# Low halves of the even sequence pieces 76 to 90: a GpSimd subtraction in place of an accumulating transfer

## The chip, the cores and the metric

One core of one Trainium2 chip. The time is the device time of one execution in microseconds (us); the kernel before took 757.11 us, the median of three runs (753.76, 757.2 and 757.11). Less is better.

## The reference

The input `x` is one batch of 2048 positions by 640 channels. The output mixes two branches by a sigmoid gate:

```python
g = sigmoid((x * gate_w).sum(-1, keepdims=True))
# A: Fourier mixing, the real part of DFT_seq(DFT_hidden(x))
a = einsum("bsd,ed->bse", x, dft_hid_re)
b = einsum("bsd,ed->bse", x, dft_hid_im)
y = einsum("ts,bse->bte", dft_seq_re, a) - einsum("ts,bse->bte", dft_seq_im, b)
# B: 32 heads choose 2 of 256 experts by product keys
q = einsum("nd,dhc->nhc", x, w_q)           # halves q1, q2
s1, s2 = q1 @ k1.T, q2 @ k2.T               # 16 scores each
# the 2 best of each half, the 2 best of their 4 sums, softmax over these 2
act = gelu(einsum("nd,nhkd->nhk", x, u[top_e]))
out = einsum("nhk,nhk,nhkd->nd", softmax(top_s), act, v[top_e])
result = g * y + (1 - g) * out
```

## The kernel before, in words

Matrix products run on TensorE with 32-bit operands that are each the sum of a high half h (the value rounded to the short form `fp32r`) and a low half l = f - h. `mm3` (lines 143 to 145) makes three matmuls of each product: h by h, h by l and l by h. Every operand therefore needs a split: ScalarE writes h with a rounding copy (line 138), and VectorE or GpSimd writes l = f - h with a subtraction (line 139). The names of the profile: `wf` is the raw piece as it came from memory, `WS` holds the halves.

**The pieces.** The sequence transforms `wsre` and `wsim` are cut in 128 pieces of 128 rows by 512 columns; piece n is used in step n of the main loop (`seq_piece`). A step asks for piece n + 5 (`load_piece`, five buffers `wf`, queue SP), splits piece n + 3 (`split_piece`, four slots `WS`), and gives TensorE the 15 matmuls of piece n. Pieces 0 to 63 are the real part, 64 to 127 the imaginary part.

**Two ways to the low half.** Either `split` (lines 138 and 139): ScalarE writes h, GpSimd subtracts. Or the accumulating way (lines 188 to 191): ScalarE writes h (line 188), ScalarE writes -h into the slot of l (line 189), and a transfer issued from the GpSimd queue reads the piece from memory once more and adds it to that slot (line 191). A condition on n chooses. With `N0` = 30, `N1` = 66, `NT` = 16 and `ACCUM_END` = 92, the pieces 34 to 63 and the even ones from 76 to 90 go the accumulating way in the kernel before.

**What runs beside the pieces.** A `Pump` holds the background work of the other engines as generators; each yield tells an estimated time of VectorE, and after each group of matmuls `run_bg` takes as many of them as the time that TensorE has used allows. So the order of the instructions on every engine is fixed when the program is built; at run time the engines wait for one another by semaphores. From about piece 76 on, that work is `experts`: `build` makes three VectorE products of 128 x 1024 in 16-bit numbers (line 803, tiles `hot`, two or four sets of buffers), `use` multiplies three such sets on TensorE (48 small matmuls, line 815), `mask` scales their result on ScalarE (line 773), and `add_up` sums it on VectorE (line 779, tile `cd`). Before a build of a new set the sums of earlier ones are put in between, so VectorE waits for ScalarE at line 779, and TensorE for VectorE at line 815.

```python
for o, a, b, op in ((pt, row(0), wt, OP.is_equal), (qt, row(1), wt, OP.is_equal), (pt, pt, row(2), OP.mult)):
    nc.vector.tensor_tensor(o, a, b, op=op)
    yield (0.8 if early else 1.05) + settle()
```

`early` holds up to piece 91. The same ScalarE queue also carries `put_rows` (line 697), which empties a buffer into which SP's next transposing transfers (line 692) write, and SP's queue carries the loads of `wf` behind these. GpSimd also splits `draw` into `DD` (128 x 640, line 139) in this stretch.

Of the kernel before, what the change touches and what calls it, by code (L numbers as in the profile page):

```python
# [25 lines left out]
NT = S // P  # L26
# [17 lines left out]
ACCUM_END = NT * (NC + 2) - 4  # L44
# [62 lines left out]
def gated_mix_kernel(ctx: ExitStack, tc: tile.TileContext, xT, xn, dreT, dimT, wsre, wsim, wq, kT, uT, vv, gw, out):  # L107
# [28 lines left out]
    def split(f, h, l, eng):  # L136

        nc.scalar.activation(h, f, AF.Copy)  # L138
        eng.tensor_sub(l, f, h.bitcast(F32))  # L139
# [29 lines left out]
    N0 = 3 * NG + 6  # L169
# [11 lines left out]
    def split_piece(n):  # L181
        if n < NPC:
            psp[n] = h, l = WS[:, n % 4, 0], WS[:, n % 4, 1]
            f = pf.pop(n)
            if not N0 + 4 <= n < (4 * NT if n % 2 else ACCUM_END) or 4 * NT <= n < N1 + 10:
                split(f, h, l, nc.gpsimd)
                return
            nc.scalar.activation(h, f, AF.Copy)
            nc.scalar.activation(l, h.bitcast(F32), AF.Copy, scale=-1.0)  # L189
            w, c, s = pieces[n]  # L190
            nc.gpsimd.dma_start(l, (wsre, wsim)[w][c, s], accum_op=OP.add)  # L191
# [37 lines left out]
    def seq_piece(n):  # L229
        w, c, s = pieces[n]  # L230
        if s == 0:
            banks[:] = [bank(d) for d in range(KD)]
        load_piece(n + 5)
        split_piece(n + 3)
        h, l = psp.pop(n)
        if n < BYPASS:
            for a, (x, c) in enumerate(((0, h), (0, l), (1, h)) if n == 0 else ((0, h), (1, h), (0, l))):
                for d in range(KD):
                    nc.tensor.matmul(banks[d], X[s][:, x, d * P:(d + 1) * P], c, start=n + a == 0, stop=False)  # L239
            return  # L240
        for d in range(KD):
            ds = slice(d * P, (d + 1) * P)
            mm3(banks[d], X[s][:, 0, ds], X[s][:, 1, ds], h, l, s == 0, s == NT - 1)
            if s == NT - 1:
                staged[n // NT, d] = f = stage()
                nc.scalar.activation(f, banks[d], AF.Copy)
            run_bg(0.68)

    for q in range(2 * NC):
        n = NT * (q + 1)  # L250
# [66 lines left out]
    for n in (1, 2):  # L317
        split_x(n)
        split_piece(n)
# [158 lines left out]
    n = b + 2  # L478
# [254 lines left out]
    for p in range(NP):  # L733
        n = N0 + 4 * p + p // 2
        for a in range(4):
            at(n + 1 + a, score_step, p, a)
    N1 = n + 5
# [266 lines left out]
    for k, (n, m) in enumerate(((-1, 2), (0, 4), (5, 7), (7, 9), (10, 12))):  # L1004
        n, m = NT * (NC + 2) + n, NT * (NC + 2) + m
# [252 lines left out]
```

## Time and profile before

| | |
|---|---|
| runs | 753.76, 757.2, 757.11 us; median 757.11 |
| profiled execution | 755.74 us, of it the span of the profile 753.0 us |
| TensorE busy | 747.6 us (99%) |
| VectorE busy | 586.1 us (78%) |
| ScalarE busy | 361.3 us (48%) |
| GpSimd busy | 347.2 us (46%) |
| accumulating transfers | 30 of `wsre` and 8 of `wsim`, 256 KB each |

The span is what the profile sees between the first and the last instruction; 2.74 us of the profiled execution lie around it. All times inside the profile are counted from the start of the span. The eight accumulating transfers of `wsim` (pieces 76 to 90) are issued between 403.2 and 459.3 us. A row of the timeline gives the start, the duration, the engine, the line and the tiles of an instruction, and in brackets how long the engine stood idle before it and what ended that.

### The profile page before, as it was taken

What the parts mean: (1) busy time and instruction counts of PE and PEld (TensorE: products, weight loads), DVE (VectorE), ACT (ScalarE), POOL (GpSimd) and SP (SyncE); (2) the same over time, 40 slices, a digit from 0 to 9 for tenths busy, and PEclk for the clock granted to TensorE, in tenths of its full rate; (3) what the DMA queues carried; (4) which work ended last, traced back from release to release, by engine and by line L of the source; (5) the groups of instructions that cost most, each with busy time, mean ns of one, the idle gap of its engine ahead of it and who ended that gap; (6) DMA issues with size and microseconds to landing.
All of it is one profiled execution on the core that took longest, in us unless ns stands there. A gap on an engine that the chain in (4) does not pass through costs nothing.

```text
span 753.0 us, 11366 instructions
## 1 busy us (share of the span) xinstructions
PE 747.6 (99%) x4045; PEld 611.2 (81%) x4045; DVE 586.1 (78%) x741; ACT 361.3 (48%) x660; POOL 347.2 (46%) x286
## 2 busy tenths in 40 slices
PE   9999999999999999999999999999999999999998
PEld 7767777888888888888888887888888888888886
DVE  6964098278999999998999887979999974267651
ACT  4424134534345745653643687633545644443451
POOL 5533226352323423325345445644456793487252
PEclk9999999999999999999999999999999999999999
DMA  9999998568356776672496866478865789774301
GB/s 329 394 389 360 345 372 330 152 169 280 68 159 172 179 260 170 148 197 86 135 390 199 155 161 187 134 234 292 280 229 195 229 260 333 231 237 158 111 29 70
DMA packets 84488, 165.87 MB, mean 220 GB/s; under 512 B 16080, under 2 KB 23376, under 8 KB 84176
## 3 DMA queue, kind: packets, MB, share of 16 engines
q1 hardware_dynamic: 70960, 140.82, 55.7%
q0 software_dynamic: 5472, 9.96, 8.7%
q10 hardware_dynamic: 8000, 14.37, 5.2%
q8 instruction: 31, 0.51, 0.3%
q14 instruction: 25, 0.20, 0.1%
HBM read 132.46 MB, written 31.08 MB: 217 GB/s over the span
## 4 chain that ended last, share of the span: by engine, by line
PE 92%; DVE 3%; DMA 2%; ACT 1%; issue 1%; SPq 1%; ACTq 0%
PE b L143 29%; PE b L144 29%; PE b L145 29%; PE b L239 2%; PE b L365 2%; DMA wq<-in_wq 2%; PE b L815 1%; DMA wf<-in_wsim 1%; DVE ST L217 1%; DVE hot L803 1%; PE b L311 1%; ACT b L773 0%; SPq L692 0%; ACT WS L138 0%; DVE tw L139 0%
## 5 line engine op out<-in xcount | busy, mean ns | idle before, releaser
L143 PE MATMUL b<-WS,X 128*128 128x512 f32 x620 | 243.5, 393 | 0.0
L144 PE MATMUL b<-WS,X 128*128 128x512 f32 x620 | 241.5, 390 | 0.0
L145 PE MATMUL b<-WS,X 128*128 128x512 f32 x620 | 241.3, 389 | 0.0
L139 POOL TENSOR_TENSOR WS<-wf,WS 128x512 fp32r<-128x512 f32 x89 | 136.2, 1536 | 163.7 <-ACT WS L138 155.9
L143 PEld LDWEIGHTS b<-WS,X 128*128 128x128 f32 x620 | 116.4, 188 | 28.0 <-issue 3.6
L145 PEld LDWEIGHTS b<-WS,X 128*128 128x128 f32 x620 | 116.4, 188 | 24.5
L144 PEld LDWEIGHTS b<-WS,X 128*128 128x128 f32 x620 | 116.4, 188 | 23.3
L138 ACT ACTIVATE WS<-wf 128x512 fp32r<-128x512 f32 x89 | 55.6, 629 | 78.9 <-PE b L145 31.2
L139 POOL TENSOR_TENSOR WS<-ra,WS 128x512 fp32r<-128x512 f32 x39 | 55.3, 1430 | 14.9 <-ACT WS L138 14.5
L139 POOL TENSOR_TENSOR xl<-xf,xh 128x640 fp32r<-128x640 f32 x16 | 28.3, 1770 | 69.7 <-ACT xh L138 63.3
L138 ACT ACTIVATE WS<-ra 128x512 fp32r<-128x512 f32 x55 | 34.5, 631 | 50.9 <-PE b L145 34.6
L803 DVE TENSOR_TENSOR hot<-rows,wtab 128x1024 f16<-128x1024 f16 x64 | 57.7, 927 | 0.8 <-PE b L815 0.8
L548 ACT ACTIVATE sc<-b 128x512 f32<-128x512 f32 x32 | 19.2, 600 | 80.8 <-PE b L145 77.8
L191 POOL DMA_DIRECT2D WS<-in_wsre x30 | 26.4, 881 | 67.5 <-ACT WS L189 66.1
L773 ACT ACTIVATE b<-b,mask 128x128 f32<-128x128 f32 x128 | 43.0, 342 | 12.0 <-PE b L815 8.3
L139 POOL TENSOR_TENSOR WP<-ra,WP 128x512 fp32r<-128x512 f32 x18 | 26.4, 1482 | 43.2 <-ACT WP L138 43.1
L598 DVE TENSOR_TENSOR eq<-sc,mm 128x1024 f16<-128x1024 f32 x32 | 41.4, 1293 | 0.9
L605 DVE TENSOR_REDUCE tied<-eq 128x64 f32<-128x1024 f16 x32 | 39.0, 1218 | 0.9
L596 DVE TENSOR_REDUCE mm<-sc 128x64 f32<-128x1024 f32 x32 | 38.8, 1211 | 0.3
L779 DVE TENSOR_REDUCE cd<-b 128x128 f32<-128x512 f32 x32 | 21.7, 683 | 13.9 <-ACT b L773 9.7
L217 DVE SCALAR_TENSOR_TENSOR ST<-ST,grow 128x512 f32<-128x512 f32 x40 | 32.4, 872 | 0.1
L803 DVE TENSOR_TENSOR hot<-hot,rows 128x1024 f16<-128x1024 f16 x32 | 32.3, 1009 | 0.0
(203 smaller groups left out, 1480.0 us busy)
## 6 DMA issues: line engine op xcount, KB each, us to landing
wq<-in_wq SPq DMA_DIRECT2D x32, 640.0 KB, 7.0
X<-xd SPq DMA_DIRECT2D x30, 640.0 KB, 6.4
wf<-in_wsim SPq DMA_DIRECT2D x64, 256.0 KB, 4.7
wf<-in_wsre SPq DMA_DIRECT2D x63, 256.0 KB, 6.1
ra<-pd SPq DMA_DIRECT2D x47, 256.0 KB, 3.1
pd<-ST ACTq DMA_DIRECT2D x35, 256.0 KB, 5.3
WS<-in_wsre POOLq DMA_DIRECT2D x30, 256.0 KB, 5.4
xd<-X SPq DMA_DIRECT2D x9, 640.0 KB, 8.9
```

What stands on the lines that cost most here:

```text
L138: nc.scalar.activation(h, f, AF.Copy)
L139: eng.tensor_sub(l, f, h.bitcast(F32))
L143: nc.tensor.matmul(o, wh, ah, start=first, stop=False, skip_group_check=more)
L144: nc.tensor.matmul(o, wh, al, start=False, stop=False, skip_group_check=more)
L145: nc.tensor.matmul(o, wl, ah, start=False, stop=last, skip_group_check=more)
L191: nc.gpsimd.dma_start(l, (wsre, wsim)[w][c, s], accum_op=OP.add)
L217: nc.vector.scalar_tensor_tensor(f, f, -1.0 if w else 1.0, g, op0=OP.mult, op1=OP.mult)
L596: nc.vector.tensor_reduce(m, sc, op=OP.max, axis=AX.X)
L598: nc.vector.tensor_tensor(eq, sc, m[:, :, None].to_broadcast([P, HH, E]), op=OP.is_equal)
L605: nc.vector.tensor_reduce(tied[:, s, ib, :], eq, op=OP.add, axis=AX.X)
L773: nc.scalar.activation(f[:, :, n], f[:, :, n], AF.Copy, scale=mask4[:, n:n + 1])
L803: nc.vector.tensor_tensor(o, a, b, op=op)
```

## The change

The condition in `split_piece` is replaced by a shorter one. Pieces 34 to 63 still go the accumulating way; the even pieces from 76 to 90 are now split as their odd neighbours are, by ScalarE's rounding copy and GpSimd's subtraction.

```diff
-            if not N0 + 4 <= n < (4 * NT if n % 2 else ACCUM_END) or 4 * NT <= n < N1 + 10:
+            if not N0 + 4 <= n < 4 * NT:
                 split(f, h, l, nc.gpsimd)
                 return
             nc.scalar.activation(h, f, AF.Copy)
             nc.scalar.activation(l, h.bitcast(F32), AF.Copy, scale=-1.0)
             w, c, s = pieces[n]
             nc.gpsimd.dma_start(l, (wsre, wsim)[w][c, s], accum_op=OP.add)
```

`ACCUM_END` keeps its value and still ends `early`. The order of TensorE's and VectorE's instructions stays as it was; the rows of two engines change.

On GpSimd, at the pieces 76 to 80 (`WS` the low half, `wf` the raw piece, `DD` the split of `draw`), before (-) and now (+):

```order
-L191 DMA WS<-in_wsim 128x512
-L139 TENSOR_TENSOR WS<-wf,WS 128x512
+L139 TENSOR_TENSOR WS<-wf,WS 128x512 x2
 L139 TENSOR_TENSOR DD<-draw,DD 128x640
-L191 DMA WS<-in_wsim 128x512
-L139 TENSOR_TENSOR WS<-wf,WS 128x512
-L191 DMA WS<-in_wsim 128x512
+L139 TENSOR_TENSOR WS<-wf,WS 128x512 x3
 L139 TENSOR_TENSOR DD<-draw,DD 128x640
```

Each transfer has become a subtraction at the same place in the queue, so that two or three subtractions now stand between two splits of `DD`.

On ScalarE, at piece 76 (line 138 the rounding copy that makes h, line 188 the same copy in the accumulating way, line 189 its copy with the sign turned):

```order
 L138 ACTIVATE WS<-wf 128x512 x3
 L138 ACTIVATE DD<-draw 128x640
-L188 ACTIVATE WS<-wf 128x512
-L189 ACTIVATE WS<-WS 128x512
+L138 ACTIVATE WS<-wf 128x512
 L666 ACT_TABLE_LOAD
 L666 ACTIVATE cc<-cc 128x128
```

The copy with the turned sign is gone here, and in the same way at the other seven pieces; nothing else in the queue has moved.

## The prediction

> **What bounds the kernel now.** I read the page first, then the busy time by windows around the eight changed pieces, then who waits for whom there, then the timelines of the five engines.
>
> ```profile
> PE 747.6 (99%) x4045; PEld 611.2 (81%) x4045; DVE 586.1 (78%) x741; ACT 361.3 (48%) x660; POOL 347.2 (46%) x286
> 402.00:422.00 20.00, 20.00 (x104) 16.33 (x103) 19.59 (x36) 7.94 (x13) 10.40 (x8) 1.00 0.94 212
> 422.00:442.00 20.00, 20.00 (x174) 16.47 (x167) 15.58 (x25) 17.06 (x37) 8.90 (x7) 1.00 0.55 123
> 442.00:462.00 20.00, 20.00 (x176) 16.25 (x175) 15.38 (x22) 15.72 (x30) 6.99 (x6) 1.00 0.80 234
> 462.00:482.00 20.00, 19.41 (x129) 15.76 (x128) 20.00 (x19) 12.77 (x32) 16.93 (x11) 1.00 0.32 87
> PE b L815 <- DVE hot L803: 0.6, 1, 0.6
> DVE cd L779 <- ACT b L773: 8.9, 4, 4.2
> ```
>
> TensorE is the bound: 747.6 of 753.0 us. The columns of a window are its length, then TensorE, its weight loads, VectorE, ScalarE, GpSimd, the granted clock, the DMA share and GB/s. From 402 to 462 us TensorE has no idle time at all, and the clock is full. So nothing that is taken off another engine there can be won on TensorE, except the one wait of 0.6 us for VectorE's `hot` near 471 us. But VectorE is nearly as full: 19.59 of 20 before 422 us, then two windows with room, which is its 8.9 us of waiting for ScalarE's masks, and 20.00 of 20 after 462 us. The question is what the change does to VectorE, and whether TensorE notices.
>
> **What the change removes.** Eight copies with turned sign on ScalarE and eight transfers issued by GpSimd.
>
> ```profile
> L189 ACT ACTIVATE WS<-WS x38: 631/633/635, 132.2 to 458.2; 128x512 fp32r<-128x512 f32 x38
> L191 POOL DMA_DIRECT2D WS<-in_wsim x8: 863/888/903, 403.2 to 459.3; - x8
> DMA to landing us min/median/max: 4.1/4.8/7.8
> ```
>
> That is 8 x 0.63 = 5.1 us of ScalarE, 8 x 0.89 = 7.1 us of GpSimd, and 8 reads of 256 KB. ScalarE's share lies beside TensorE's work except in one chain (below). A piece is also ready sooner, since a subtraction replaces a transfer that lands 4.8 us later, but TensorE never waited for these pieces, so that is worth nothing.
>
> **What it adds.** Eight GpSimd subtractions of 128 x 512.
>
> ```profile
> L139 POOL TENSOR_TENSOR WS<-wf,WS x89: 1280/1533/2344, 8.1 to 589.5; 128x512 fp32r<-128x512 f32 x89
> 412.43 1.51 POOL L139 TENSOR_TENSOR WS<-wf,WS 128x512 fp32r<-128x512 f32 x1 [1.53 <-ACT WS L138]
> 412.11 2.39 DVE L803 TENSOR_TENSOR hot<-rows,wtab 128x1024 f16<-128x1024 f16 x2
> 415.02 1.28 DVE L803 TENSOR_TENSOR hot<-rows,wtab 128x1024 f16<-128x1024 f16 x2
> 425.32 0.90 POOL L191 DMA_DIRECT2D WS<-in_wsim  x1 [4.36 <-ACT WS L189]
> 425.64 1.28 DVE L803 TENSOR_TENSOR hot<-rows,wtab 128x1024 f16<-128x1024 f16 x2
> ```
>
> GpSimd itself has room: 8 x 1.53 = 12.2 us less the 7.1 removed. VectorE pays. Two products of line 803 take 1.28 us when GpSimd is quiet (415.02), and also while it issues a transfer (425.64); they take 2.39 us when a GpSimd subtraction runs beside them (412.11). So each subtraction costs VectorE 1.11 us, a transfer's issue nothing. From below the cost of one is 0, where VectorE idles or runs an instruction that isn't blocked:
>
> ```profile
> 463.37 3.44 POOL L139 TENSOR_TENSOR WS<-wf,WS 128x512 fp32r<-128x512 f32 x2
> 463.87 0.68 DVE L779 TENSOR_REDUCE cd<-b 128x128 f32<-128x512 f32 x1
> ```
>
> The sum of line 779 keeps its 0.68 us inside two subtractions. The Trainium skill, "SBUF — State Buffer", section "Who interferes with whom", has the rule that speaks against this change: a VectorE instruction with two inputs in SBUF contends with a GpSimd instruction that reads SBUF, a reduction doesn't, and the loser is blocked until the other has finished. The rows agree on who is blocked; on the length they show 1.11 us, where a whole undisturbed subtraction lasts 1.28. With 1.28 for each the result below would be 2.9 instead of 2.4 us.
>
> **The first group: three subtractions that nothing absorbs.** Pieces 76, 78 and 80 are split while VectorE works without a gap towards the first `use`.
>
> ```profile
> 400.39 1.56 POOL L139 TENSOR_TENSOR DD<-draw,DD 128x640 fp32r<-128x640 f32 x1
> 400.45 1.78 DVE L609 TENSOR_TENSOR first<-tied,top_bits 128x256 int32<-128x256 int32 x1
> 401.51 0.63 ACT L188 ACTIVATE WS<-wf 128x512 fp32r<-128x512 f32 x1 [2.14 <-issue]
> 403.40 0.42 DVE L609 TENSOR_TENSOR tied<-tied,top_bits 128x256 int32<-128x256 int32 x1
> 408.31 0.63 ACT L188 ACTIVATE WS<-wf 128x512 fp32r<-128x512 f32 x1 [1.41 <-POOL WS L139]
> 409.86 0.95 DVE L671 RECIPROCAL cc<-cc 128x128 f32<-128x128 f32 x1
> 415.06 0.63 ACT L188 ACTIVATE WS<-wf 128x512 fp32r<-128x512 f32 x1 [2.72 <-PE b L145]
> 416.22 0.68 DVE L803 TENSOR_TENSOR hot<-hot,rows 128x1024 f16<-128x1024 f16 x1
> 419.73 1.78 DVE L803 TENSOR_TENSOR hot<-hot,rows 128x1024 f16<-128x1024 f16 x1
> 421.75 0.95 PE L815 MATMUL b<-hot 128*64 128x64 f16 x48
> 422.63 0.50 PE L143 MATMUL b<-WS,X 128*128 128x512 f32 x1
> ```
>
> The three rows of line 188 give the moment from which each subtraction can start. Piece 76 (402.14 on) meets small VectorE operations with two inputs; line 609 shows that they are blocked too (1.78 us beside a split of `DD`, 0.42 without), so 1.1. Piece 78 (408.94 on, and behind 77 and a split of `DD` in GpSimd's queue, so nearer 410) meets mostly one-input operations such as the reciprocal, for which no row shows a block: between 0 and 1.1, and I take 0.5. Piece 80 (415.69 on) meets line 803: 1.1. VectorE is then 1.1 + 0.5 + 1.1 = 2.7 us late. The third set of the first group was finished at 419.73 + 1.78 = 421.51 us; its 16 matmuls are the last third of the 48 that fill 421.75 to 422.63, so they began at 422.34. Slack 0.8 us. TensorE waits 2.7 - 0.8 = 1.9 us.
>
> **The middle: absorbed.** Pieces 82 to 88 cost VectorE up to 4.4 us more, but it had 8.9 us of waiting there, and the waits are set by ScalarE, whose masks follow TensorE's own matmuls. The longest of them ends a chain:
>
> ```profile
> 436.94 1.47 ACT L773 ACTIVATE b<-b,mask 128x128 f32<-128x128 f32 x4 [1.25 <-PE b L815]
> 439.79 0.63 ACT L189 ACTIVATE WS<-WS 128x512 fp32r<-128x512 f32 x1
> 443.08 1.93 ACT L697 ACTIVATE rows<-lb 128x384 f16<-128x384 f16 x1
> 445.04 3.64 SPq L692 DMA_TRANSPOSE lb<-lb  x3
> 448.72 2.58 SPq L177 DMA_DIRECT2D wf<-in_wsim  x4
> 454.28 0.63 ACT L138 ACTIVATE WS<-wf 128x512 fp32r<-128x512 f32 x1 [3.49 <-DMA wf<-in_wsim]
> 456.30 0.69 DVE L779 TENSOR_REDUCE cd<-b 128x128 f32<-128x512 f32 x1 [4.18 <-ACT b L773]
> ```
>
> TensorE's second group frees ScalarE at 436.94; ScalarE then works without a gap to line 697 (443.08), SP's transposes wait for that (445.04), the next load of `wf` stands behind them (448.72), ScalarE waits for it (454.28), and its masks release VectorE (456.30). In the changed kernel this chain starts 1.9 us late with TensorE and loses the 0.63 us of one copy (439.79). VectorE restarts 1.3 us late whatever it lost in between.
>
> **The end of the stretch.** From there VectorE has no gap until TensorE's wait:
>
> ```profile
> 457.57 0.62 ACT L188 ACTIVATE WS<-wf 128x512 fp32r<-128x512 f32 x1
> 469.26 1.77 DVE L803 TENSOR_TENSOR hot<-hot,rows 128x1024 f16<-128x1024 f16 x1
> 471.09 0.44 PE L815 MATMUL b<-hot 128*64 128x64 f16 x16 [0.59 <-DVE hot L803]
> ```
>
> Piece 90 (458.19 on) meets line 803 again and adds 1.1, so the set that ended at 469.26 + 1.77 = 471.03 comes 1.3 + 1.1 = 2.4 us later. TensorE waited for it already before, so it now goes on 2.4 us later than before; 1.9 of this it had lost at the first group. Behind this place all engines are late by the same amount, and TensorE, full, gives nothing back.
>
> **The sum.** +2.4 us. On the profiled execution (753.0 of span and 2.74 around it, 755.74) that makes 758.1; the median of the runs lies 1.4 higher, and the measured time is a median, so I give 757.1 + 2.4 = 759.5. The unknown prices move it from +0.8 (of these only pieces 80 and 90 block: 1.1 - 0.8 = 0.3 at the first group, 0.3 - 0.6 = -0.3 at the chain, -0.3 + 1.1 = 0.8 at the end) to +3.0 (piece 78 at its full 1.1).
>
> **Rivals.** *Nothing is absorbed.* VectorE becomes the bound for the whole stretch: the subtractions stack up, all eight at 1.1 us, 8.8 less the 0.8 of slack, +8.0 us, which is 763.7 on the profiled execution. For it: 20.00 of 20 after 462 us, and the estimated 0.8 us per `build` instruction, less than the 0.88 us that VectorE's row group
>
> ```profile
> L803 DVE TENSOR_TENSOR hot<-rows,wtab 128x1024 f16<-128x1024 f16 x28 | 23.7, 879 | 0.0
> ```
>
> shows on average even with the transfers. Against it: the 8.9 us of waiting in between. It passes 0.5% (3.8 us) once five of the eight reach TensorE, since 5 x 1.1 - 0.8 = 4.7: the three of the first group at full price and two of the last, for instance where the wait for `wf` at 454 us is shorter and VectorE's gap of 4.18 us goes. *The cover holds.* The early subtractions fall on unblocked operations and the removed copies bring the chain forward by 0.6 us: the wait at 471.09 goes, -0.6 us, 755.1 on the profiled execution. Against it: line 803 at pieces 80 and 90. *The transfers were in the way.* Without the accumulating reads the loads of `wf` come sooner and the slower runs become like the fastest, 753.8. Against it: TensorE stands still for just 0.59 us in the whole stretch, so the profile offers no such gain. That the change does nothing is excluded: GpSimd's and ScalarE's queues differ at eight places.
>
> **Chances.** A measurement of this kernel tells about 0.5%, 3.8 us, from no change. My case, +0.3 to +3.8 us: 0.44. Nothing or less absorbed, over +3.8 us: 0.42, high because each further blocked instruction of line 803 in the full windows goes straight into TensorE's wait, and because every error of my count that I can name (a second subtraction beside the same build, less waiting at line 779) points that way. The cover holds: 0.08. The transfers were in the way: 0.06. So slower by over 0.5% 0.42, within it 0.44 + 0.08 = 0.52, faster 0.06. The range goes from 755.1, the cover's time, to 763.7, the time of the rival without absorption; it leaves out the faster case and what of the slower one lies higher.
>
> **What would show it.** In the profile after: TensorE's wait for `hot` at the first use of line 815 near 422 us, about 1.9 us, and a second, 0.5 to 1.1 us long, near 473 us; line 803's mean between 402 and 462 us above 0.88 us; VectorE's wait at line 779 shorter than 8.9 us; line 773 released by the load of `wf` near 456 us; the stretches before 402 and after 480 us unchanged in length. Wrong it is if TensorE's first wait is missing, if waits appear at the groups near 436 or 448 us, or if TensorE's idle time grows where no line 815 stands.

## The result, and the profile after

The changed kernel takes 758.07 us in the median of 18 runs (756.42 to 760.92), the kernel before 754.81 us in the median of 18 (753.76 to 758.09): a ratio of 1.0038, 95% interval 1.0027 to 1.0049, or +2.9 us (2.0 to 3.7). It is slower, by less than the 0.5% that the prediction took as its bound. The forecast was +2.4 us, inside the interval. As a time it was 759.5 us, 1.4 too long, since it was counted from the median of only three runs of the kernel before, 757.11 us, which lies 2.3 above the median of all 18. The profiled execution took 757.59 us with a span of 755.8.

The first line of the page after, and the four windows of the prediction (length, then TensorE, weight loads, VectorE, ScalarE, GpSimd, granted clock, DMA share, GB/s):

```profile
PE 748.3 (99%) x4045; PEld 611.7 (81%) x4045; DVE 596.1 (79%) x741; ACT 356.6 (47%) x652; POOL 350.9 (46%) x286
402.00:422.00 20.00, 20.00 (x90) 16.57 (x89) 19.59 (x31) 6.53 (x10) 12.78 (x9) 1.00 0.58 183
422.00:442.00 20.00, 18.64 (x169) 14.99 (x168) 20.00 (x26) 13.18 (x28) 8.10 (x5) 1.00 0.21 60
442.00:462.00 20.00, 20.00 (x151) 16.18 (x151) 20.00 (x23) 16.64 (x32) 11.88 (x8) 1.00 0.69 225
462.00:482.00 20.00, 19.13 (x165) 15.65 (x159) 20.00 (x21) 11.97 (x31) 13.70 (x9) 1.00 0.31 87
```

VectorE is busy for 10.0 us more in all, though its instructions are the same 741, and from 422 to 482 us it has no idle time left; before, it had 9.0 us of it between 422 and 462. TensorE has lost 1.36 us in the second window. Where, the timeline of TensorE shows, at the first group of line 815 and at the fifth:

```profile
422.67 0.83 PE L815 MATMUL b<-hot 128*64 128x64 f16 x32
424.86 0.44 PE L815 MATMUL b<-hot 128*64 128x64 f16 x16 [1.36 <-DVE hot L803]
472.31 0.69 PE L815 MATMUL b<-hot 128*64 128x64 f16 x32
473.88 0.44 PE L815 MATMUL b<-hot 128*64 128x64 f16 x16 [0.87 <-ACT b L773]
```

Two thirds of the first group run at once, the last third waits for VectorE's product. Without the wait it would have begun 0.59 us after the group, at 423.26; so the group loses 1.6 us. At the fifth group the wait of before, 0.59, has grown to 0.87. (The name behind it, line 773, is the last release in the profile; VectorE's product ended at 473.83.) These two places make about 1.8 us of the 2.8 between the two spans. The rest lies ahead of any changed instruction, in TensorE's waits for `wq` at the start of the kernel: 0.9 us here, 0.4 in the profile before, and 0.5 us within the first 6 us.

### The profile page after: what moved, and what is told of

It reads as the page before. It is cut to its first block, busy times and chain, and to the rows that moved or that the text cites. A ratio compares the mean times of both kernels' runs of the same rounds, so it can differ in the third digit from the quotient of the medians.

```text
span 755.8 us, 11360 instructions
## 1 busy us (share of the span) xinstructions
PE 748.3 (99%) x4045; PEld 611.7 (81%) x4045; DVE 596.1 (79%) x741; ACT 356.6 (47%) x652; POOL 350.9 (46%) x286
## 4 chain that ended last, share of the span: by engine, by line
PE 85%; DVE 12%; DMA 2%; issue 1%; ACT 0%; SPq 0%; DVEq 0%
PE b L143 27%; PE b L144 26%; PE b L145 26%; PE b L239 2%; PE b L365 2%; DMA wq<-in_wq 2%; DVE eq L598 1%; DVE mm L596 1%; DVE hot L803 1%; PE b L815 1%; DVE ST L217 1%; DVE eq L603 1%; DVE tied L605 1%; DVE sc L601 1%; PE b L311 1%
## 5 line engine op out<-in xcount | busy, mean ns | idle before, releaser
L139 POOL TENSOR_TENSOR WS<-wf,WS 128x512 fp32r<-128x512 f32 x97 | 146.9, 1519 | 174.8 <-ACT WS L138 173.0
L138 ACT ACTIVATE WS<-wf 128x512 fp32r<-128x512 f32 x97 | 60.7, 629 | 87.2 <-PE b L145 35.7
L803 DVE TENSOR_TENSOR hot<-rows,wtab 128x1024 f16<-128x1024 f16 x64 | 67.5, 1080 | 0.8 <-PE b L815 0.8
L143 PE MATMUL b<-WU,xh 128*128 128x512 f32 x80 | 31.2, 391 | 0.0
```

The lines of the kernel that those rows point to most:

```text
L143: nc.tensor.matmul(o, wh, ah, start=first, stop=False, skip_group_check=more)
```

## The experiments

Each ran in rounds with the kernel before on the same chip. "Lost" below is how much later TensorE's instructions start than in a trace of the kernel before, counted only behind 400 us, so that the start of the kernel is left out.

**Both kernels once more.**

> The changed kernel unaltered, for a second trace. The first trace shows 1.6 us lost at the first group and 0.2 us more near 474 us, 1.8 us in all, where the medians differ by 2.9 us. If the missing 1.1 us lies at the same two places in other executions, this trace shows over 2.2 us there; if they repeat to 0.3 us, the rest is in the transfers at the start of the kernel, which differ between executions. Ratio 1.003 to 1.005.

> The kernel before unaltered, for a second trace. Ratio 1.000. No wait at the first group near 422 us; the wait near 471 us of 0.6 us either repeats or shows how much it differs between executions; the waits for wq between 107 and 121 us differ by more than that.

The changed kernel: 758.18 us, ratio 1.0046 (1.0032 to 1.0061). The kernel before against its own other runs: 1.0009 (0.9998 to 1.0021). TensorE in the second trace of the changed kernel, and then in the second trace of the kernel before, at the fifth group:

```profile
424.02 0.84 PE L815 MATMUL b<-hot 128*64 128x64 f16 x32
426.22 0.44 PE L815 MATMUL b<-hot 128*64 128x64 f16 x16 [1.36 <-DVE hot L803]
473.81 0.55 PE L815 MATMUL b<-hot 128*64 128x64 f16 x24
475.16 0.44 PE L815 MATMUL b<-hot 128*64 128x64 f16 x16 [0.81 <-DVE hot L803]
```

```profile
470.82 0.95 PE L815 MATMUL b<-hot 128*64 128x64 f16 x48
```

The first group's wait repeats, 1.36 us in both. The wait at the fifth group is not a fixed part of the kernel before: 0.59 in its first trace, none in its second. Between the second traces the changed kernel loses 1.6 us at the first group and 1.0 at the fifth, 2.6 in all; between the first traces it was 1.8. The second lies inside the measured +2.0 to +3.7 us, the first 0.2 below it. TensorE's waits for `wq` were 2.1 and 1.0 us in this pair; they are what differs most between executions, and a remainder of 0.3 to 1 us isn't told apart from them.

**One part of the change alone.** In `e1_first` the condition ends `4 * NT <= n < N1 + 16`, in `e2_last` the even pieces go the accumulating way up to `N1 + 16`:

```diff
-            if not N0 + 4 <= n < (4 * NT if n % 2 else ACCUM_END) or 4 * NT <= n < N1 + 10:
+            if not N0 + 4 <= n < (4 * NT if n % 2 else ACCUM_END) or 4 * NT <= n < N1 + 16:   # e1_first
+            if not N0 + 4 <= n < (4 * NT if n % 2 else N1 + 16) or 4 * NT <= n < N1 + 10:     # e2_last
```

> Pieces 76, 78 and 80 by subtraction as in the changed kernel, 82 to 90 by accumulating transfers as before. Lock theory (each GpSimd subtraction blocks a two-input VectorE operation for 1.1 us, and TensorE loses only where a set of hot falls due): TensorE's wait at the first group near 423 us is there, about 1.6 us; VectorE is set right again by ScalarE's masks in the middle; +1.6 us on the kernel before. Even-share rival (each of the eight costs the same part of the measured 2.9 us): 3 x 0.37 = +1.1 us, and no particular wait. Transfer rival (the loss comes with the transfers and copies that are taken away): also 3 x 0.37 = +1.1 us, with a wait that is not at line 815.

> Pieces 76, 78 and 80 by accumulating transfers as before, 82 to 90 by subtraction as in the changed kernel. Lock theory: no wait at the first group; five locks of 1.1 us fall into VectorE's 8.9 us of waiting at line 779, so TensorE's wait near 471 us grows from 0.6 to between 0.9 and 1.7 us: +0.3 to +1.1 us. Even-share rival: 5 x 0.37 = +1.8 us.

`e1_first` 757.59 us, ratio 1.0035 (1.0022 to 1.0049); `e2_last` 756.14 us, ratio 1.0013 (1.0001 to 1.0025). TensorE's waits for VectorE, first in `e1_first`, then in `e2_last` (us in total, times, longest):

```profile
PE b L815 <- DVE hot L803: 1.4, 1, 1.4
```

```profile
PE b L815 <- DVE hot L803: 1.2, 1, 1.2
```

In `e1_first` it is the wait at the first group, with the same 1.36 us and 1.55 lost; the fifth group has no wait, as in the second trace of the kernel before. In `e2_last` the first group has no wait, and the one at the fifth is 1.18 us: 0.5 lost against the first trace of the kernel before, which waits there too, and 1.4 against the second, which doesn't. By the runs, three of the eight subtractions cost +2.6 us (1.7 to 3.7) and the other five +1.0 (0.1 to 1.9). An even share would have made it +1.1 and +1.8. The first figure speaks against the even-share rival, the second is too wide to; more telling is that each wait stands at the group behind its own pieces and at no other. The figure of `e1_first` is 1 us above what was expected; its trace shows no more than the expected loss behind 400 us, and long waits for `wq` (3.1 us) ahead of any changed instruction, so that difference stays open.

**The subtraction without taking anything away, and taking away without the subtraction.** In `e3_dummy` (first part of the diff) a subtraction is added ahead of each of the eight transfers; in `e4_none` (second part) the eight low halves are left out.

```diff
+            if n >= 4 * NT:
+                nc.gpsimd.tensor_sub(f, f, h.bitcast(F32))
             nc.gpsimd.dma_start(l, (wsre, wsim)[w][c, s], accum_op=OP.add)
...
+            if n >= 4 * NT:
+                return
             nc.scalar.activation(l, h.bitcast(F32), AF.Copy, scale=-1.0)
```

> The kernel before with all of its transfers and copies, and beside each of the eight accumulating transfers of pieces 76 to 90 one more GpSimd subtraction of 128 x 512, whose result (written over the raw piece) nobody uses. Lock theory: what is added is the whole cost: +1.9 to +2.9 us, with a wait of 1.6 us or a little more at the first group. Transfer rival: nothing is taken away, so 0.

> The low halves of the even pieces 76 to 90 are left out: neither transfer, nor copy with turned sign, nor subtraction; the slots keep older low halves. Lock theory: no lock and less on ScalarE, so between -0.6 us (the wait near 471 us goes) and 0. Transfer rival: the loss comes with what is taken away, so about +2.9 us.

`e3_dummy` 759.49 us, ratio 1.0057 (1.0045 to 1.0069), +4.3 us; `e4_none` 755.45 us, ratio 1.0004 (0.9994 to 1.0014), no difference that can be measured. Adding the subtractions alone makes the kernel slower, taking the transfers and copies away alone does nothing that can be measured: the transfer rival falls. But `e3_dummy` costs more than expected, and not all of it is the subtractions' price. TensorE's waits in it, by line and cause (two lines were added above, so line 817 is the former 815 and 805 the former 803):

```profile
PE b L817 <- DVE hot L805: 1.7, 2, 1.0
PE b L144 <- DMA WS<-in_wsim: 1.1, 1, 1.1
```

The second wait is new: the transfers now stand behind the added subtractions in GpSimd's queue, one of them landed too late for its piece, and TensorE stood 1.15 us for it near 420 us and lost 1.4. That one isn't VectorE's, and it takes part of what the first group's wait would have been (0.73 us there). Without these 1.4 us the trace has lost 1.5 us behind 400 us against the first trace of the kernel before and 2.4 against the second, which is near the changed kernel's loss. The changed kernel has no such transfers.

**More of the same.** `e6_double` makes each of the eight subtractions twice:

```diff
                 split(f, h, l, nc.gpsimd)
+                if n % 2 == 0 and 4 * NT + 12 <= n < ACCUM_END:
+                    nc.gpsimd.tensor_sub(f, f, h.bitcast(F32))
                 return
```

> The changed kernel with each of the eight GpSimd subtractions made twice, the second over the raw piece and unused. Lock theory with slack: VectorE has no idle time left from 422 us on in the changed kernel, so each of the eight further locks of 1.1 us reaches TensorE: 8 to 9 us over the changed kernel, +10 to +12 us on the kernel before; the first group's wait rises from 1.4 to about 4.5 us. Even-share rival: twice the loss, +5.8 us.

766.21 us, ratio 1.0161 (1.0139 to 1.0183), +12.2 us: far from twice 2.9, so the second lock costs much more than the first, as when the slack is used up. The first group's three waits add to 4.9 us (1.07, 1.36 and 2.43; the lines stand two further down here too). But the sum came out as expected partly for another reason. Behind the longest wait TensorE itself ran slow (matmuls at the first group and after, then windows with the granted clock in the third column from the end):

```profile
429.72 0.64 PE L817 MATMUL b<-hot 128*64 128x64 f16 x16 [2.43 <-DVE hot L805]
430.29 0.80 PE L143 MATMUL b<-WS,X 128*128 128x512 f32 x1
430.88 0.63 PE L144 MATMUL b<-WS,X 128*128 128x512 f32 x1
```

```profile
426.00:430.00 4.00, 0.72 (x26) 0.61 (x28) 4.00 (x6) 1.47 (x4) 2.31 (x2) 0.90 0.25 74
430.00:434.00 4.00, 4.00 (x23) 3.17 (x20) 4.00 (x6) 1.19 (x2) 0.79 (x1) 0.50 0.23 66
434.00:438.00 4.00, 4.00 (x15) 3.19 (x14) 2.75 (x5) 2.50 (x5) 0.00 (x1) 0.75 0.00 0
```

Counted in the trace, 8.4 us are lost in waits for VectorE and 4.3 us in stretches at half clock behind waits of 2.43 and 2.35 us. So the waits grew from about 2.6 to 8.4 us, 5.8 for eight further locks, less than the 8 to 9 expected: while TensorE was slow, VectorE found idle time again (one wait of 3.1 us at the former line 779).

**Another engine for the subtraction.** `e5_vector` puts the eight on VectorE:

```diff
-                split(f, h, l, nc.gpsimd)
+                split(f, h, l, nc.vector if n % 2 == 0 and 4 * NT + 12 <= n < ACCUM_END else nc.gpsimd)
```

> The eight subtractions of the changed kernel on VectorE in place of GpSimd. A VectorE subtraction of this size takes 0.69 us in the trace, 0.6 from start to start; a GpSimd one blocks VectorE for 1.1 us. Lock theory: VectorE is late by 3 x 0.6 = 1.8 us at the first group instead of 2.4, less 0.8 of slack: a wait of 1.0 us there, and +0.5 to +1.5 us in all, less than the changed kernel. Rival (the place in VectorE's queue matters, since it must wait for ScalarE's copy): VectorE stands still at line 139 and it is slower than the changed kernel, +3 us or more.

757.35 us, ratio 1.0033 (1.0021 to 1.0045), +2.5 us, above the expected +0.5 to +1.5 and not told apart from the changed kernel. The lines of VectorE in it between 400 and 465 us (minimum, median and maximum in ns), and what it waited for:

```profile
L139 DVE TENSOR_TENSOR WS<-wf,WS x8: 677/680/1787, 410.4 to 457.2; 128x512 fp32r<-128x512 f32 x8
DVE WS L139 <- ACT WS L138: 2.2, 2, 1.4
```

Six of the eight take the expected 0.68 us, and the first group's wait is 0.60 us with 0.8 lost instead of 1.6. But two, at 413 and 441 us, meet other GpSimd work and take 1.79 and 1.64 us, and VectorE twice stood waiting for ScalarE's copy at its own subtraction, 2.2 us. TensorE lost another 0.5 us at the group near 449 us, and at the one near 471 us 1.0 against the second trace of the kernel before, 0.2 against the first. The rival had part of it right: the place in the queue takes back some of what the lower price gives.

**What a GpSimd instruction with one input costs.** In `e8_one_input` GpSimd multiplies h by -1 in place of the subtraction, so that the low halves of these pieces hold -h:

```diff
+                if n % 2 == 0 and 4 * NT + 12 <= n < ACCUM_END:
+                    nc.scalar.activation(h, f, AF.Copy)
+                    nc.gpsimd.tensor_scalar(l, h.bitcast(F32), -1.0, None, op0=OP.mult)
+                    return
                 split(f, h, l, nc.gpsimd)
```

> The changed kernel with the eight GpSimd subtractions replaced by a GpSimd multiplication of h by -1, which reads one tensor in place of two and writes the same 128 x 512 (so the low halves of these eight pieces hold -h). Lock theory with the block lasting as long as GpSimd reads: blocks of about half the length if the time follows the number of tensors read, a wait of under 0.5 us at the first group and 0 to +1 us in all; if any GpSimd instruction that reads blocks for 1.1 us, +2.9 us as in the changed kernel; if an instruction with one input doesn't block, 0.

756.52 us, ratio 1.0020 (1.0008 to 1.0032), +1.5 us, and no wait at the first group. GpSimd's instruction at piece 80 and VectorE's two products beside it (line 807 is the former 803):

```profile
416.15 1.94 POOL L188 TENSOR_SCALAR WS<-WS 128x512 fp32r<-128x512 f32 x1 [2.11 <-ACT WS L187]
416.06 1.70 DVE L807 TENSOR_TENSOR hot<-rows,wtab 128x1024 f16<-128x1024 f16 x2
```

The two take 1.70 us, where an undisturbed pair takes 1.28 and a pair beside a subtraction 2.39. So this instruction blocks VectorE for 0.42 us against 1.11, though it lasts no less long itself; beside six of the eight, one operation of VectorE is longer by 0.41 to 0.43 us. The price does not follow the length of GpSimd's instruction. That it follows the number of tensors read is likely and not shown alone, since the operation is another one too. Of the +1.5 us the trace shows 0.2 behind 400 us against the first trace of the kernel before and 1.1 against the second, there at the fifth group (a wait of 0.74 us); the rest stays open.

**Taking more away.** `e7_more` lets six more even pieces, 92 to 102, go the accumulating way (`ACCUM_END + 12` in the condition).

> The kernel before, with the even pieces 92 to 102 by accumulating transfers too, six more than before. Lock theory: six locks of 1.1 us less between 463 and 500 us, but TensorE there waits for VectorE only 0 to 0.6 us, so -0.6 to 0 us. Rival (each lock that is taken away gives its share, 0.37 us): -2.2 us.

755.56 us, ratio 1.0005 (0.9993 to 1.0017). Its trace has no wait of TensorE at line 815 at all, and that brings nothing that can be measured: the second trace of the kernel before has none either. No version here beats the kernel before.

## Why the prediction was right, point by point

**The bound.** TensorE stays the bound; its lost time is the result. Right.

**The price of a subtraction.** 1.11 us on VectorE was right where a blocked operation lies beside the whole subtraction; three of the last five, which fall in part on the sums of line 779, cost 0.5 to 0.7 us. That the removed transfers and copies are worth nothing was right (`e4_none`).

**The first group.** VectorE's operations at pieces 76 and 78 in the profile after, with GpSimd's subtraction of 78 between them:

```profile
403.19 1.52 DVE L626 TENSOR_TENSOR tied<-tied,first 128x256 f32<-128x256 f32 x1
411.24 1.34 POOL L139 TENSOR_TENSOR WS<-wf,WS 128x512 fp32r<-128x512 f32 x1
411.36 1.45 DVE L660 COPY lb<-lb 128x256 f16<-128x256 f16 x2
412.98 0.95 DVE L671 RECIPROCAL cc<-cc 128x128 f32<-128x128 f32 x1
416.94 1.78 DVE L803 TENSOR_TENSOR hot<-hot,rows 128x1024 f16<-128x1024 f16 x1
424.13 0.68 DVE L803 TENSOR_TENSOR hot<-hot,rows 128x1024 f16<-128x1024 f16 x1
```

Piece 76 cost 1.1 (line 626 took 0.42 before), piece 80 another 1.1 (line 803, 0.68 before), both as predicted. Piece 78, put at 0.5, cost its full 1.1: it met the 16-bit copy of line 660, whose two copies took 0.35 us before and now 1.45. The subtraction of piece 79 began at 413.33, inside the reciprocal, which took its 0.95 as before. With the start of the kernel 0.92 us later, the third set ended at 424.81 instead of 422.43: 2.4 us late, not 3.3, because the shift let two other locks fall on cheaper places. So the sum of 2.7 was 0.3 too high, the slack of 0.8 was right, and the wait, predicted as 1.9 us, was 1.6.

**The middle.** This step failed. The prediction let VectorE restart at line 779 when ScalarE's masks came, behind the late load of `wf`. The row that answers to 456.30:

```profile
454.86 0.63 ACT L138 ACTIVATE WS<-wf 128x512 fp32r<-128x512 f32 x1 [1.02 <-DMA wf<-in_wsim]
455.79 0.68 DVE L779 TENSOR_REDUCE cd<-b 128x128 f32<-128x512 f32 x1
```

ScalarE waits 1.02 us for `wf` instead of 3.49, and VectorE doesn't wait at line 779 at all, here or at any other place of the stretch: its 8.9 us of waiting are gone. The locks of the last five subtractions don't fill them alone. Between the first and the fifth group, 18 operations of VectorE are longer than the shortest of their kind, each of them beside a subtraction of GpSimd, by 17.2 us together; in the kernel before it was 8.1 us. The five new subtractions make only 3.9 us of this, since three of them fall in part on those sums. The other 13.3 us, 5 more than before, come from GpSimd work that the change leaves alone. One case, first in the kernel before, then in the changed one:

```profile
428.06 1.55 POOL L139 TENSOR_TENSOR DD<-draw,DD 128x640 fp32r<-128x640 f32 x1 [1.83 <-ACT DD L138]
429.87 0.69 DVE L779 TENSOR_REDUCE cd<-b 128x128 f32<-128x512 f32 x1 [2.35 <-ACT b L773]
```

```profile
430.28 1.85 POOL L139 TENSOR_TENSOR DD<-draw,DD 128x640 fp32r<-128x640 f32 x1 [3.72 <-ACT DD L138]
430.04 2.65 DVE L803 TENSOR_TENSOR hot<-rows,wtab 128x1024 f16<-128x1024 f16 x2
```

Before, this split of `DD` ran while VectorE waited and cost it nothing; now it meets two products and costs 2.65 - 1.28 = 1.37 us. So VectorE's idle time had hidden locks of the old work, and the prediction, which counted only the new ones, had no term for these. VectorE is the late one from then on: of the 2.4 us carried in, 1.9 are left at the fifth group. The chain that was worked out in such detail does not set the time there. Where the last five subtractions are missing, in `e1_first`, VectorE still waits 6.2 us at line 779 and TensorE doesn't wait at the fifth group: there the step holds.

**The fifth group.** Predicted +0.5 us beyond the first group's 1.9; the traces show +0.2 and +1.0 beyond 1.6. The size was near, the way to it was not: that the sum came out near the measured +2.9 us is in part luck. And the predicted range of +0.8 to +3.0 us hid that the wait of 0.59 us before was itself no constant.

**The rivals.** *Nothing is absorbed* (+8.0) is refuted for eight locks, but the idle time that spoke against it is used up: `e6_double` shows what the next eight do. *The cover holds* and *the transfers were in the way* are refuted by `e3_dummy` and `e4_none`.

## What to carry to other kernels

Where VectorE runs close behind TensorE, a GpSimd instruction beside it is to be priced by what it takes from VectorE, not by GpSimd's own busy share: a subtraction of 128 x 512 here cost VectorE 1.1 us, more than the 0.68 us that the same subtraction takes on VectorE. Count such locks from the last place where VectorE had idle time to the next place where TensorE needs its result, and take off the slack there; three of the eight pieces made most of this loss. Where the new locks use up VectorE's idle time, count also the old locks that it had hidden. And take a second trace of the kernel before: a wait that is in one and not in the other is no term of a sum.

## What the runs showed of the hardware

Two things were not expected. First, a GpSimd instruction that lasts 1.94 us blocked VectorE for 0.42 us when it read one tensor, while one that lasts 1.3 to 1.5 us and reads two blocked it for 1.1. The Trainium skill, "SBUF — State Buffer", section "SBUF: two separate sides", says that the loser is blocked for the whole instruction; here the block was shorter than the instruction as the profile shows it in both cases, and the measured prices stand. The Trainium skill, on the same page, section "Who interferes with whom", names copies among the operations that can take part in it, which the two copies of line 660 bear out.

Second, TensorE's granted clock fell to half after single waits of 2.03 us and more, but not after those of up to 1.6 us (the longest, 1.61 us for `wq` in `e6_double`, kept the full clock). Beside the two cases of `e6_double`, two of the waits for `wq` at the start show it, one of 2.06 us in `e1_first` and here the one in `e4_none`, with windows of 4 us:

```profile
109.05 1.07 PE L367 MATMUL b<-wq,kp 128*32 128x320 f32 x8 [2.03 <-DMA wq<-in_wq]
108.00:112.00 4.00, 2.95 (x13) 1.74 (x14) 3.42 (x9) 1.90 (x6) 0.00 (x0) 0.67 0.90 323
112.00:116.00 4.00, 4.00 (x17) 3.22 (x16) 1.36 (x3) 1.58 (x5) 0.85 (x1) 0.91 0.81 268
```

The two windows lack 0.33 and 0.09 of the clock; at half clock that is 2 x 4 x 0.42 = 3.4 us. The three windows of `e6_double` give 2 x 4 x (0.10 + 0.50 + 0.25) = 6.8 us in the same way, two such stretches. The Trainium skill, "TensorE: Matmul & The Clock Gate", section "HAM oscillation — how this bites in real kernels", puts the limit at gaps of about 3.4 us; here a gap of 2.03 us was enough. What lies between 1.6 and 2.0 us, and whether it is the one wait or the idle share of a longer stretch that counts, is not shown. The changed kernel's wait of 1.36 us stays below that: its windows show the full clock, and it pays for the wait alone.
